# Accumulating DMAs in place of GpSimd additions in a channel attention with a rational feed-forward network

## The chip, the core and the metric

The kernel runs on one NeuronCore of one Trainium2 chip. The engines are named as the profile names them: PE is TensorE (matmuls), PEld its weight loads, DVE is VectorE, ACT is ScalarE, POOL is GpSimd, SP is SyncE, which here only issues DMAs. The metric is the time of one execution on the device, in microseconds (us).

## The reference

Two parts follow one another. For each of 4 batches with 6080 rows of 256 channels, a channel attention is computed, and its 24320 output rows then pass a feed-forward network whose activation is a quotient of two polynomials:

```python
qn = q / (norm(q, axis=1) + 1e-06);  kn = k / (norm(k, axis=1) + 1e-06)   # norms over the 6080 rows
s = kn.transpose(0, 2, 1) @ qn / tau                                       # 256 x 256 per batch
a = softmax(s);  x = (v @ a).reshape(24320, 256)
h = x @ w_in                                                               # 24320 x 2048
P = a0 + a1 * h + a2 * h**2 + a3 * h**3
Q = 1 + abs(b0) * abs(h) + abs(b1) * h**2
out = (P / (Q + 1e-06)) @ w_out                                            # 24320 x 256
```

## The kernel before

**Tiles.** The rows go in groups of 512 (the last of each batch has 448): 12 groups in each of 4 batches, 48 in all. The 2048 hidden channels go in 8 pairs of 128-channel blocks, pair 0 to pair 7, so there are 384 steps "group and pair" (function `pair`, line 620). The softmax matrix of a batch is multiplied into `w_in` first (`fuse`, line 560), so that h comes straight from v.

**One pair.** PE makes h of 256 channels by 512 rows into a PSUM tile `hx` (three such tiles, `hx0` to `hx2`) with 12 matmuls, called mm1 here. Then, with all tiles 128 x 1024:

- ACT "first": d = hx squared. POOL "line": d = d * |b1| + 1. ACT "second": uu = |b0 * hx|. POOL "sum": d = d + uu. That is the denominator Q. In pairs 1, 3 and 6 (`FACTORED`, line 252) it is made in another way, without a sum: ACT "first" uu = |b1 * hx|, DVE a product, ACT "abs", and later POOL "one", which adds the 1.
- ACT "slope": uu = a3 * hx + a2; DVE twice makes the numerator in hx ("num1", "num2").
- ACT "root" and "square": r = 1/d to the precision of the table. POOL "again": d = d * r. DVE "quot": hx = hx * r; DVE "last": g = (2 - d) * hx, a step of Newton's method. Only then is the hx tile free for the mm1 of another pair.
- PE multiplies g with `w_out` into `acc` (4 matmuls with two records each, in two halves), called the out product here; at the end of a group DVE turns acc and SP stores it.

**The attention of batch 0** stands at the start (24 halves of 256 rows of k and q: load, PE products, ACT square into one of two tiles `sq`, addition of the squares into one tile by POOL or DVE). The attention of batches 1 to 3 is spread over the pairs of the batch before (`Attn.half`, line 423); 12 halves of batch 1, called fronts, are pulled into the start. There POOL adds each square tile into `ssq` (line 464). The softmax of a batch (line 475) needs the finished ssq.

**What sets the order.** Every step is given to a planner (`Planner`, line 83) with an engine, a cost, what it reads and writes, and a due time: the step's row of `LAG` or `TIME` (lines 21 to 45) on top of 3.576 us per pair. The planner replays the engines and puts on each, whenever it is free, the ready step with the smallest due time. What comes out is a fixed order on each engine; on the chip each engine runs its rows in that order and waits for semaphores. So a new number in the table can reorder all five engines. There are also three hx, four d, four uu, three r, four g and two sq tiles; a step that needs a new tile waits until one is free.

Of the kernel before, what the change touches and what calls it, by code (L numbers as in the profile page):

```python
# [14 lines left out]
ALU = mybir.AluOpType  # L15
# [3 lines left out]


LAG = {
    "first": (0.84, 4.52, 2.78, 3.73, 4.53, 2.33, 3.41, 3.6),
    "prod": (-11.23, -0.03, -11.23, 6.14, -11.23, -11.23, 5.27, -11.23),
    "abs": (-35.28, -33.04, -35.28, -60.18, -35.28, -35.28, -12.39, -35.28),
    "line": (-60.83, 30.85, 1.23, -9.96, -64.93, -61.3, 25.68, -3.97),
    "second": (3.47, 5.1, 5.85, 6.25, 8.47, 6.18, 3.15, 4.97),
    "sum": (-75.1, -80.53, -59.16, -66.42, -83.56, -73.41, -47.34, -36.63),
    "slope": (6.9, 4.95, 7, 7.41, 9.07, 6.95, 6.12, 6.22),
    "num1": (80.21, 21.96, 120.89, 23.72, 98.59, 65.28, 53.4, 94.99),
    "num2": (91.21, 77.02, 48.39, 83.69, 132.26, 79.9, 92.26, 66.3),  # L30
    "root": (-17.03, -9.24, -6.87, -5.73, -6.19, -9.62, -12.27, -14.71),
    "one": (18.62, -22.45, 18.62, 2.61, 18.62, 18.62, 25.53, 18.62),
    "square": (-78.86, -34.07, -129.08, -42.44, -147.95, -117.98, -7.49, -107.82),
    "again": (-10.9, -52.88, -8.31, -23.6, -7.9, 6.38, -36.31, -6.49),
    "quot": (38.4, 26.11, 35.76, 10.27, 43.7, 29.95, 4.71, 41.91),
    "last": (-3.36, 0.17, -3.01, -4.4, 0.77, 1.56, -1.89, -4.37),
    "out": (24.58, 54.15, 41.53, 45.99, 18.94, 61.33, 13.35, 15.28),
    "in": (-5.72, -5.59, -3.14, -6.52, -2.09, -4.66, -7.12, -10.04), "in_n": 0,
}
TIME = {  # L40
    "pair": 3.576, "start": 61.026, "load": 1.674, "softmax": 52.628, "in": 4.243, "late_in": 1.499,
    "out0": 30.295, "out": 5.035, "attn0_0": -1.487, "attn_0": 1.155, "attn0": 4.026, "attn": 1.97,
    "attn1": 91.474, "value": 54.159, "fuse": 1.698, "finish": 21.052, "front": 41.363,
    "front_pace": 1.762, "ahead": 15.518, "vhi": 26.968, "vlo": 25.086,
}


# [29 lines left out]


class Step:
    __slots__ = ("eng", "cost", "fn", "key", "need", "after", "new", "bufs", "banks", "port", "n")  # L80


class Planner:
# [14 lines left out]
        self.slots, self.fifo, self.banks = slots, fifo, banks  # L98
        self.steps = []

    def add(self, eng, cost, key, fn, reads=(), writes=(), port=False):
        s = Step()
        s.eng, s.cost, s.fn, s.key = eng, cost, fn, key
# [24 lines left out]
        for w in before.values():  # L128
            w.after.append(s)
        self.steps.append(s)  # L130
        return s

    def order(self):
# [29 lines left out]
        while left:  # L163
            for e in ready:
                while busy[e] <= now and ready[e]:
                    skipped, pick = [], None
                    while ready[e]:
                        entry = heapq.heappop(ready[e])
                        if fits(entry[2]):
                            pick = entry[2]  # L170
                            break
                        skipped.append(entry)
                    for entry in skipped:
                        heapq.heappush(ready[e], entry)
                    if pick is None:
                        break
                    for b in pick.new:
                        b.slot = free[b.tag].pop(0)
                        if b.tag in queue:
                            queue[b.tag].pop()  # L180
                    out.append((now, pick))
                    left -= 1
                    busy[e] = now + pick.cost
                    if pick.port:
                        other = "POOL" if e == "DVE" else "DVE"
                        busy[e] = max(now, port[other]) + pick.cost
# [11 lines left out]
            while events and events[0][0] <= now:  # L198
                _, what, _, s = heapq.heappop(events)
# [17 lines left out]
def tile_channel_attention_rational_ffn(  # L217
# [43 lines left out]
    pool = InOrder(tc, nc.gpsimd)  # L261
# [139 lines left out]
    class Attn:  # L401
# [21 lines left out]
        def half(self, i, at, both, sps):  # L423
# [3 lines left out]
            base, pn = groups[g]  # L427
# [31 lines left out]
            else:  # L459
# [160 lines left out]
    def pair(m, at, vparts, w, acc):  # L620
# [9 lines left out]
        def c(b):  # L630
            return b[:, :, :n]
# [21 lines left out]
        else:  # L653
# [121 lines left out]
```

## Time and profile before

| | us |
|---|---|
| median of 2 runs | 2647.04 |
| the two runs | 2646.86 and 2647.22 |
| span of the profiled execution | 2645.5 |

| engine | busy us | share of the span |
|---|---|---|
| PE | 2595.5 | 98% |
| DVE | 2259.8 | 85% |
| POOL | 2216.3 | 84% |
| ACT | 2124.2 | 80% |

The profiled execution's span runs from its first to its last instruction; the runs' times hold about 1.5 us more. The busy time of PE is modelled for pipelined matmuls. Issuing a DMA is not counted as busy. The profile gives tile names without their numbers, and nearly every instruction stands on one helper's line (L58), so rows are told apart by tile names. The views read here are the page's parts, the table of busy times by stretch, the chain of work that ended last, the timeline of an engine, and the list of DMA issues with their time to landing.

### The profile page before, as it was taken

How to read it: one execution, taken by the hardware profiler on the slowest of the kernel's cores; microseconds unless marked ns; L12 is line 12 of the kernel's file. 1: busy time of each engine (PE TensorE's matmuls, PEld its weight loads, DVE VectorE, ACT ScalarE, POOL GpSimd, SP SyncE). 2: the span in 40 equal slices, each digit the busy share in tenths (PEclk: the TensorE clock that was granted, in tenths of full speed). 3: DMA queues.
4: the chain of work that ended last, by engine and by line, in shares of the span. 5: the costliest groups of instructions: out<-in, count | busy, mean ns of one | idle time of the engine just before them, and what ended most of it. 6: DMA issues, size and time to landing. Idle time of an engine off the chain costs nothing.

```text
span 2645.5 us, 26474 instructions
## 1 busy us (share of the span) xinstructions
PE 2595.5 (98%) x8744; PEld 1651.8 (62%) x8744; DVE 2259.8 (85%) x2035; ACT 2124.2 (80%) x2179; POOL 2216.3 (84%) x1152
## 2 busy tenths in 40 slices
PE   7899999999999999999999999999999999999998
PEld 6656666666666666666666666665666566666665
DVE  6898888988978787888888878888897889889887
ACT  5688888888878778788878778778887888888886
POOL 6889888888778999788878899878885888888886
PEclk9899999999999999999999999999999999999999
DMA  9512311111112222211121222211111111111101
GB/s 306 153 25 64 68 19 25 23 17 24 17 35 53 48 65 53 48 24 17 23 40 16 49 68 51 46 25 17 23 25 17 18 22 24 22 18 25 23 9 15
DMA packets 457017, 109.76 MB, mean 41 GB/s; under 512 B 405168, under 2 KB 453808, under 8 KB 456880
## 3 DMA queue, kind: packets, MB, share of 16 engines
q1 hardware_dynamic: 456880, 108.07, 19.4%
q8 instruction: 69, 1.13, 0.2%
q14 instruction: 68, 0.56, 0.1%
HBM read 83.10 MB, written 24.90 MB: 41 GB/s over the span
## 4 chain that ended last, share of the span: by engine, by line
PE 88%; ACT 4%; DVE 3%; DMA 2%; issue 1%; POOL 1%; SPq 0%; DVEq 0%; ACTq 0%; POOLq 0%
PE acc L58 45%; PE hx L58 43%; ACT uu L58 1%; DVE hx L58 1%; DMA r<-in_k_dram 1%; ACT r L58 1%; ACT d L58 1%; POOL d L58 0%; DVE uu L58 0%; DMA r<-in_q_dram 0%; DMA kq<-in_k_dram 0%; SPq L58 0%; ACT sq L58 0%; DVE g L58 0%; POOL ssq L58 0%
## 5 line engine op out<-in xcount | busy, mean ns | idle before, releaser
L58 PE MATMUL acc<-g,w_out_sb 128*128 128x512 f32 (+1 forms) x3072 | 1349.7, 588 | 4.5 <-DVE orow L58 4.4
L58 POOL TENSOR_TENSOR d<-d,r 128x1024 f32<-128x1024 f32 (+1 forms) x384 | 906.5, 2364 | 166.9 <-ACT r L58 155.0
L58 PE MATMUL hx<-vhi,w 128*128 128x512 f32 (+1 forms) x3072 | 961.4, 420 | 7.4 <-DVE g L58 5.3
L58 PEld LDWEIGHTS acc<-g,w_out_sb 128*128 128x128 f32 x3072 | 581.2, 189 | 618.6 <-issue 592.4
L58 PEld LDWEIGHTS hx<-vhi,w 128*128 128x128 f32 x3072 | 578.2, 189 | 229.4 <-issue 94.3
L58 POOL TENSOR_TENSOR d<-d,uu 128x1024 f32<-128x1024 f32 (+1 forms) x243 | 575.6, 2369 | 35.0 <-ACT uu L58 20.5
L58 DVE TENSOR_TENSOR uu<-uu,hx 128x1024 f32<-128x1024 f32 (+1 forms) x384 | 462.4, 1204 | 149.9 <-ACT uu L58 148.8
L58 DVE SCALAR_TENSOR_TENSOR hx<-hx,coef,r 128x1024 f32<-128x1024 f32 (+1 forms) x384 | 489.2, 1275 | 111.3 <-ACT r L58 106.9
L58 ACT ACTIVATE d<-hx 128x1024 f32<-128x1024 f32 (+1 forms) x243 | 247.1, 1017 | 345.7 <-PE hx L58 338.6
L58 DVE SCALAR_TENSOR_TENSOR hx<-uu,coef,hx 128x1024 f32<-128x1024 f32 (+1 forms) x384 | 487.7, 1273 | 4.2
L58 DVE SCALAR_TENSOR_TENSOR g<-d,hx 128x1024 f32<-128x1024 f32 (+1 forms) x384 | 461.0, 1201 | 21.6 <-POOL d L58 15.0
L58 PE MATMUL hx<-vlo,w 128*128 128x512 f32 (+1 forms) x1536 | 473.7, 390 | 0.0
L58 ACT ACTIVATE uu<-hx,babs 128x1024 f32<-128x1024 f32 (+1 forms) x384 | 425.9, 1109 | 50.7 <-PE hx L58 50.7
L58 ACT ACTIVATE uu<-hx,coef 128x1024 f32<-128x1024 f32 (+1 forms) x384 | 461.4, 1201 | 1.3 <-DVE d L58 1.3
L58 ACT ACTIVATE r<-d 128x1024 f32<-128x1024 f32 (+1 forms) x384 | 405.4, 1056 | 20.2 <-POOL d L58 17.8
L58 ACT ACTIVATE r<-r 128x1024 f32<-128x1024 f32 (+1 forms) x384 | 405.2, 1055 | 6.8
L58 POOL TENSOR_SCALAR d<-d,babs 128x1024 f32<-128x1024 f32 (+1 forms) x243 | 272.2, 1120 | 133.8 <-ACT d L58 130.7
L58 PEld LDWEIGHTS hx<-vlo,w 128*128 128x128 f32 x1536 | 288.9, 188 | 60.7
L58 DVE SCALAR_TENSOR_TENSOR d<-uu,babs,hx 128x1024 f32<-128x1024 f32 (+1 forms) x141 | 178.2, 1264 | 33.7 <-ACT uu L58 33.4
L58 POOL TENSOR_SCALAR d<-d,ones 128x1024 f32<-128x1024 f32 (+1 forms) x141 | 157.5, 1117 | 36.7 <-ACT r L58 36.6
L58 POOL TENSOR_TENSOR ssq<-sq,ssq 128x1024 f32<-128x1024 f32 (+1 forms) x69 | 166.0, 2406 | 24.0 <-ACT sq L58 19.5
L58 ACT ACTIVATE d<-d 128x1024 f32<-128x1024 f32 (+1 forms) x141 | 146.8, 1041 | 9.8 <-DVE d L58 9.8
(82 smaller groups left out, 1119.1 us busy)
## 6 DMA issues: line engine op xcount, KB each, us to landing
vst<-in_v_dram SPq DMA_DIRECT2D x352, 64.0 KB, 2.3
out_dram<-orow SPq DMA_DIRECT2D x352, 64.0 KB, 2.0
kq<-in_k_dram SPq DMA_DIRECT2D x78, 256.0 KB, 3.8
kq<-in_q_dram SPq DMA_DIRECT2D x78, 256.0 KB, 4.2
d<-in_moe_w_in_dram SPq DMA_DIRECT2D x8, 512.0 KB, 7.0
r<-in_k_dram SPq DMA_DIRECT2D x10, 256.0 KB, 6.5
r<-in_q_dram SPq DMA_DIRECT2D x10, 256.0 KB, 6.5
d<-in_moe_w_out_dram SPq DMA_DIRECT2D x4, 512.0 KB, 8.2
```

Of the source, the lines that this page charges most:

```text
L58: ins = op(*args, **kwargs)
```

## The change

Two kinds of POOL additions become DMAs that POOL issues and that add their source to what stands in the destination: the sum of pairs 0 and 4 in every group (96 additions) and the additions of square tiles into ssq in batches 1 to 3 (69 additions). Both are 128 x 1024 in 32-bit, 512 KB (a group of 448 rows and the last two halves of a batch are a little smaller). The planner counts each of them with 1.0 on POOL, and lets its result be used 5.0 later (`SUM_LANDS`, passed as `tail`). All due times in `LAG` and `TIME` are new, so the order changes on every engine.

```diff
+    CARRIED = (0, 4)
+
+    SUM_LANDS = 5.0
...
-    def add(self, eng, cost, key, fn, reads=(), writes=(), port=False):
+    def add(self, eng, cost, key, fn, reads=(), writes=(), port=False, tail=0.0):
...
-                    heapq.heappush(events, (busy[e] + self.HOP[e], 1, pick.n, pick))
+                    heapq.heappush(events, (busy[e] + self.HOP[e] + pick.tail, 1, pick.n, pick))
                     for c, lat in enumerate(self.LAT[e].values()):
-                        heapq.heappush(events, (busy[e] + lat, 10 + c, pick.n, pick))
+                        heapq.heappush(events, (busy[e] + lat + pick.tail, 10 + c, pick.n, pick))
...
-                fn = lambda: e.tensor_tensor(total[:pn], sq[:pn], total[:pn], op=ALU.add)
-                step(*(("DVE", 1.2) if own else ("POOL", 2.38)), at + 2, fn, [sq, total], [total], True)
+                if first:
+                    fn = lambda: e.tensor_tensor(total[:pn], sq[:pn], total[:pn], op=ALU.add)
+                    step(*(("DVE", 1.2) if own else ("POOL", 2.38)), at + 2, fn, [sq, total], [total], True)
+                else:
+                    fn = lambda: pool.dma_start(out=total[:pn], in_=sq[:pn], accum_op=ALU.add)
+                    step("POOL", 1.0, at + 2, fn, [sq, total], [total], tail=SUM_LANDS)
...
-            fn = lambda: pool.tensor_tensor(c(d), c(d), c(kk), op=ALU.add)
-            step("POOL", 2.36 * s, at + LAG["sum"][p], fn, [d, kk], [d])
+            if p in CARRIED:
+                fn = lambda: pool.dma_start(out=c(d), in_=c(kk), accum_op=ALU.add)
+                step("POOL", 1.0, at + LAG["sum"][p], fn, [d, kk], [d], tail=SUM_LANDS)
+            else:
+                fn = lambda: pool.tensor_tensor(c(d), c(d), c(kk), op=ALU.add)
+                step("POOL", 2.36 * s, at + LAG["sum"][p], fn, [d, kk], [d])
```

Of the tables, two rows show the manner of the change:

```diff
-    "sum": (-75.1, -80.53, -59.16, -66.42, -83.56, -73.41, -47.34, -36.63),
+    "sum": (-76.15, -179.7, -63.44, -133.87, -63.68, -59.31, -81.78, -42.08),
-    "pair": 3.576, "start": 61.026, "load": 1.674, "softmax": 52.628, "in": 4.243, "late_in": 1.499,
+    "pair": 3.576, "start": 69.136, "load": 1.731, "softmax": 58.346, "in": 3.756, "late_in": 1.499,
```

**Place 1, the middle of batch 0, where one group's pair 7 and the next group's pair 0 stand together.** On POOL before, with pair 7 in d3 and pair 0 in d0: line and sum of 7, line of 0, a split of the next group's values (vlo), sum of 0, again of 7, again of 0.

```order
L58 TENSOR_SCALAR d3_84<-d3_84,babs_77 128x1024
L58 TENSOR_TENSOR d3_84<-d3_84,uu0_85 128x1024
L58 TENSOR_SCALAR d0_81<-d0_81,babs_77 128x1024
L58 TENSOR_TENSOR vlo0_139<-cv0_97,vhi0_137 128x1024
L58 TENSOR_TENSOR d0_81<-d0_81,uu1_86 128x1024
L58 TENSOR_TENSOR d3_84<-d3_84,r1_108 128x1024
L58 TENSOR_TENSOR d0_81<-d0_81,r2_109 128x1024
```

On POOL now, with pair 0 in d3 and pair 7 in d0:

```order
L59 TENSOR_SCALAR d3_84<-d3_84,babs_77 128x1024
L59 TENSOR_SCALAR d0_81<-d0_81,babs_77 128x1024
L59 DMA d3_84<-uu0_85 128x1024
L59 TENSOR_TENSOR d0_81<-d0_81,uu3_88 128x1024
L59 TENSOR_TENSOR vlo0_139<-cv0_97,vhi0_137 128x1024
L59 TENSOR_TENSOR d0_81<-d0_81,r1_108 128x1024
L59 TENSOR_TENSOR d3_84<-d3_84,r2_109 128x1024
```

The sum of pair 0 has become a DMA and has moved ahead of the sum of pair 7; the landing has the sum of 7, vlo and the again of 7 beside it. On ACT before, the second of pair 0 (`uu1<-hx1,babs`) and its root (`r2<-d0`) have five rows between them:

```order
L58 ACTIVATE uu1_86<-hx1_91,babs_77 128x1024
L58 ACTIVATE r1_108<-d3_84 128x1024
L58 ACTIVATE uu3_88<-hx1_91,coef_71 128x1024
L58 ACTIVATE r1_108<-r1_108 128x1024
L58 ACTIVATE uu0_85<-hx2_92,babs_77 128x1024
L58 ACTIVATE uu2_87<-hx2_92,coef_71 128x1024
L58 ACTIVATE r2_109<-d0_81 128x1024
```

On ACT now, the second of pair 0 (`uu0<-hx2,babs`) and its root (`r2<-d3`):

```order
L59 ACTIVATE d3_84<-hx2_92 128x1024
L59 ACTIVATE uu3_88<-hx1_91,babs_77 128x1024
L59 ACTIVATE d0_81<-hx1_91 128x1024
L59 ACTIVATE uu0_85<-hx2_92,babs_77 128x1024
L59 ACTIVATE uu1_86<-hx2_92,coef_71 128x1024
L59 ACTIVATE uu2_87<-hx1_91,coef_71 128x1024
L59 ACTIVATE vhi0_137<-cv0_97 128x1024
L59 ACTIVATE r1_108<-d0_81 128x1024
L59 ACTIVATE uu3_88<-hx0_90,babs_77 128x1024
L59 ACTIVATE r1_108<-r1_108 128x1024
L59 ACTIVATE r2_109<-d3_84 128x1024
L59 ACTIVATE d1_82<-d1_82 128x1024
```

Now six rows stand between them, among them the root and square of pair 7, and the second of pair 0 comes only after the second and first of pair 7.

**Place 2, PE at the same joint.** Before, what follows the mm1 of pair 0 in a group of batch 0 (g and w_out_sb mark out products; x4 is a whole one, x2 a half): half an out product, the mm1 of pair 1, two and a half out products, and then the mm1 of pair 2 and of pair 3, which takes over the hx tile of pair 0.

```order
L58 MATMUL acc0_89<-g0_93,w_out_sb_80 128x512 x2
L58 MATMUL hx2_92<-vhi0_137,w1_117 128x512 x2
L58 MATMUL hx2_92<-vlo0_139,w1_117 128x512 x2
L58 MATMUL hx2_92<-vhi0_137,w21_127 128x512 x2
L58 MATMUL hx2_92<-vhi0_137,w1_117 128x512 x2
L58 MATMUL hx2_92<-vlo0_139,w1_117 128x512 x2
L58 MATMUL hx2_92<-vhi0_137,w21_127 128x512 x2
L58 MATMUL acc0_89<-g0_93,w_out_sb_80 128x512 x2
L58 MATMUL acc0_89<-g3_96,w_out_sb_80 128x512 x4
L58 MATMUL acc0_89<-g1_94,w_out_sb_80 128x512 x4
```

Now the mm1 of pair 0 of the next group is followed by the mm1 of pair 7 of this one (not shown), then by these rows, then by the mm1 of pair 2 and of pair 3, which again takes over the hx tile of pair 0:

```order
L59 MATMUL acc0_89<-g2_95,w_out_sb_80 128x512 x2
L59 MATMUL acc0_89<-g3_96,w_out_sb_80 128x512 x2
L59 MATMUL hx0_90<-vhi1_138,w1_117 128x512 x2
L59 MATMUL hx0_90<-vlo1_140,w1_117 128x512 x2
L59 MATMUL hx0_90<-vhi1_138,w21_127 128x512 x2
L59 MATMUL hx0_90<-vhi1_138,w1_117 128x512 x2
L59 MATMUL hx0_90<-vlo1_140,w1_117 128x512 x2
L59 MATMUL hx0_90<-vhi1_138,w21_127 128x512 x2
L59 MATMUL acc0_89<-g3_96,w_out_sb_80 128x512 x2
L59 MATMUL acc0_89<-g0_93,w_out_sb_80 128x512 x4
L59 MATMUL acc0_89<-g1_94,w_out_sb_80 128x512 x4
```

One mm1 and half an out product have come between pair 0's mm1 and pair 3's: before three mm1 and three out products, now four mm1 and three and a half.

**Place 3, POOL at the start.** Now the additions of the fronts (ssq) and the first pairs stand like this; each ssq row reads and writes the same tile as the one before it:

```order
L59 DMA ssq0_142<-sq1_106 128x1024
L59 TENSOR_TENSOR vlo0_139<-cv0_97,vhi0_137 128x1024
L59 DMA ssq0_142<-sq0_105 128x1024
L59 DMA ssq0_142<-sq1_106 128x1024
L59 TENSOR_SCALAR d0_81<-d0_81,babs_77 128x1024
L59 DMA d0_81<-uu0_85 128x1024
L59 DMA ssq0_142<-sq0_105 128x1024
L59 TENSOR_SCALAR d1_82<-d1_82,babs_77 128x1024
L59 DMA ssq0_142<-sq1_106 128x1024
L59 TENSOR_TENSOR d0_81<-d0_81,r0_107 128x1024
```

Before, the eleven additions of the fronts were POOL work of the same kind as its other additions; now each row is a DMA, and a row that adds into ssq waits on POOL for the landing of the one before it.

## Rows read from the trace of the kernel before

**Rows 1.** The page, part 1: span, and busy time of PE.

```profile
span 2645.5 us, 26474 instructions
PE 2595.5 (98%) x8744; PEld 1651.8 (62%) x8744; DVE 2259.8 (85%) x2035; ACT 2124.2 (80%) x2179; POOL 2216.3 (84%) x1152
```

**Rows 2.** Busy time by stretch: stretch, length, each engine's, PE clock, DMA share, GB/s.

```profile
0.00:57.20 57.20, 43.88 (x184) 35.80 (x184) 40.18 (x57) 31.12 (x34) 39.47 (x24) 1.00 0.97 305
57.20:114.40 57.20, 46.24 (x186) 37.57 (x186) 50.88 (x69) 37.83 (x50) 41.16 (x18) 0.91 0.74 226
114.40:171.60 57.20, 50.43 (x159) 32.01 (x159) 49.69 (x46) 42.19 (x46) 53.00 (x27) 0.91 0.12 19
...
sum 2637.20, PE 2594.85 PEld 1651.75 DVE 2258.68 ACT 2124.22 POOL 2216.33; mean PE 185.35 PEld 117.98 DVE 161.33 ACT 151.73 POOL 158.31
```

**Rows 3.** The chain that ended last, one group: start, length, engine, tile, count.

```profile
2182.53 5.49 PE hx L58 x24
2188.03 3.43 PE acc L58 x8
...
2231.94 5.49 PE hx L58 x24
```

**Rows 4.** The page, part 5: costliest groups, busy, mean ns, idle before, its releaser.

```profile
L58 POOL TENSOR_TENSOR d<-d,r 128x1024 f32<-128x1024 f32 (+1 forms) x384 | 906.5, 2364 | 166.9 <-ACT r L58 155.0
L58 POOL TENSOR_TENSOR d<-d,uu 128x1024 f32<-128x1024 f32 (+1 forms) x243 | 575.6, 2369 | 35.0 <-ACT uu L58 20.5
...
L58 DVE SCALAR_TENSOR_TENSOR g<-d,hx 128x1024 f32<-128x1024 f32 (+1 forms) x384 | 461.0, 1201 | 21.6 <-POOL d L58 15.0
...
L58 POOL TENSOR_TENSOR ssq<-sq,ssq 128x1024 f32<-128x1024 f32 (+1 forms) x69 | 166.0, 2406 | 24.0 <-ACT sq L58 19.5
```

**Rows 5.** Timeline of ACT at the joint of pairs 7 and 0: start, length.

```profile
2189.25 1.13 ACT L58 ACTIVATE uu<-hx,babs 128x1024 f32<-128x1024 f32 x1
2190.24 1.23 ACT L58 ACTIVATE uu<-hx,coef 128x1024 f32<-128x1024 f32 x1
2191.33 1.09 ACT L58 ACTIVATE r<-d 128x1024 f32<-128x1024 f32 x1
2192.28 1.09 ACT L58 ACTIVATE vhi<-cv 128x1024 fp32r<-128x1024 f32 x1
2193.23 1.09 ACT L58 ACTIVATE r<-r 128x1024 f32<-128x1024 f32 x1
2194.24 1.11 ACT L58 ACTIVATE uu<-hx,babs 128x1024 f32<-128x1024 f32 x1
2195.25 1.05 ACT L58 ACTIVATE r<-d 128x1024 f32<-128x1024 f32 x1
```

**Rows 6.** DMA issues, 800 to 1750 us: count, KB each, median us to landing.

```profile
kq<-in_k_dram SPq DMA_DIRECT2D x38, 256.0 KB, 3.5
kq<-in_q_dram SPq DMA_DIRECT2D x38, 256.0 KB, 3.9
...
vst<-in_v_dram SPq DMA_DIRECT2D x128, 64.0 KB, 2.3
```

**Rows 7.** Timeline of SP's queue: start and length of two issues.

```profile
870.45 0.37 SPq L58 DMA_DIRECT2D kq<-in_k_dram  x1
870.87 0.46 SPq L58 DMA_DIRECT2D kq<-in_q_dram  x1
```

**Rows 8.** The page, part 6: DMA issues of 512 KB at the start.

```profile
d<-in_moe_w_in_dram SPq DMA_DIRECT2D x8, 512.0 KB, 7.0
...
d<-in_moe_w_out_dram SPq DMA_DIRECT2D x4, 512.0 KB, 8.2
```

**Rows 9.** The chain at the start: additions of two fronts on it.

```profile
90.54 2.45 POOL ssq L58
...
93.06 2.70 POOL ssq L58
```

**Rows 10.** Timeline of POOL at the start: front additions ahead of sums.

```profile
105.83 2.36 POOL L58 TENSOR_TENSOR ssq<-sq,ssq 128x1024 f32<-128x1024 f32 x1 [0.82 <-ACT sq L58]
108.14 2.81 POOL L58 TENSOR_TENSOR d<-d,uu 128x1024 f32<-128x1024 f32 x1
...
112.20 2.34 POOL L58 TENSOR_TENSOR ssq<-sq,ssq 128x1024 f32<-128x1024 f32 x1
```

More of the change, by code (lines that the diff above doesn't have):

```diff
@@ L21 @@
 LAG = {
[L22 to L26, printed above, removed]
-    "sum": (-75.1, -80.53, -59.16, -66.42, -83.56, -73.41, -47.34, -36.63),
-    "slope": (6.9, 4.95, 7, 7.41, 9.07, 6.95, 6.12, 6.22),
-    "num1": (80.21, 21.96, 120.89, 23.72, 98.59, 65.28, 53.4, 94.99),
@@ L30 @@
[L30 to L36, printed above, removed]
@@ L37 @@
-    "out": (24.58, 54.15, 41.53, 45.99, 18.94, 61.33, 13.35, 15.28),
-    "in": (-5.72, -5.59, -3.14, -6.52, -2.09, -4.66, -7.12, -10.04), "in_n": 0,
+    "first": (-1.99, 4.49, 3.1, 3.03, 1.87, -0.28, 3.36, 6.44),
+    "prod": (-11.23, -0.46, -11.23, -0.12, -11.23, -11.23, 3.8, -11.23),
+    "abs": (-35.28, -29.57, -35.28, -8.58, -35.28, -35.28, -17.35, -35.28),
+    "line": (-122.86, 33.27, 8.62, 16.73, -76.41, -61.41, 66.33, -3.06),
+    "second": (3.74, 8.46, 5.21, 2.29, 3.83, 1.92, 2.25, 3.66),
@@ new lines @@
+    "sum": (-76.15, -179.7, -63.44, -133.87, -63.68, -59.31, -81.78, -42.08),
+    "slope": (5.31, 7.08, 5.75, 6.91, 4.8, 5.34, 5.4, 10.51),
+    "num1": (66.19, 42.24, 127.36, 40.45, 114.89, 112.9, 108.9, 121.16),
+    "num2": (64.16, 106.31, 36.31, 113.96, 151.19, 73.39, 60.59, 112.92),
+    "root": (-5.53, -6.36, -6.67, -4.44, -5.9, -3.77, -5.84, -3.96),
+    "one": (18.62, -13.08, 18.62, 46.24, 18.62, 18.62, 50.45, 18.62),
+    "square": (-78.24, -15.43, -115.55, -80.53, -183.43, -168.21, 8.84, -69.8),
@@ L39 @@
+    "again": (26.08, -26.07, -56.72, -85.22, 42.66, 72.65, 12.44, 42.65),
+    "quot": (-16.24, 29.72, 73.49, 15.23, 90.25, 57.13, 41.36, 1.68),
+    "last": (-3.16, -5.28, -5.96, -8.65, -11.31, -12.32, -9.08, -1.92),
+    "out": (-7.39, 43.1, 31.6, 151.13, 23.05, 33.84, 45.58, 72.14),
+    "in": (-12.17, -4.89, -0.56, -3.35, -0.62, -3.21, -5.76, -8.02),
+    "in_n": 0,
 }
 TIME = {
-    "pair": 3.576, "start": 61.026, "load": 1.674, "softmax": 52.628, "in": 4.243, "late_in": 1.499,
-    "out0": 30.295, "out": 5.035, "attn0_0": -1.487, "attn_0": 1.155, "attn0": 4.026, "attn": 1.97,
@@ L43 @@
-    "attn1": 91.474, "value": 54.159, "fuse": 1.698, "finish": 21.052, "front": 41.363,
-    "front_pace": 1.762, "ahead": 15.518, "vhi": 26.968, "vlo": 25.086,
+    "pair": 3.576, "start": 69.136, "load": 1.731, "softmax": 58.346, "in": 3.756, "late_in": 1.499,
+    "out0": -35.671, "out": 8.872, "attn0_0": -1.138, "attn_0": 1.117, "attn0": 4.621,
+    "attn": 1.914, "attn1": 91.638, "value": 56.407, "fuse": 2.088, "finish": 22.037,
+    "front": 55.516, "front_pace": 2.35, "ahead": -13.72, "vhi": 33.796, "vlo": 0.862,
@@ L79 @@
 class Step:
-    __slots__ = ("eng", "cost", "fn", "key", "need", "after", "new", "bufs", "banks", "port", "n")
+    __slots__ = ("eng", "cost", "tail", "fn", "key", "need", "after", "new", "bufs", "banks", "port", "n")
 class Planner:
@@ L99, in __init__ @@
         self.steps = []
-    def add(self, eng, cost, key, fn, reads=(), writes=(), port=False):
+    def add(self, eng, cost, key, fn, reads=(), writes=(), port=False, tail=0.0):
         s = Step()
-        s.eng, s.cost, s.fn, s.key = eng, cost, fn, key
+        s.eng, s.cost, s.fn, s.key, s.tail = eng, cost, fn, key, tail
         s.n = len(self.steps)
@@ L289, in buf, with step @@
         return Buf(tag, view)
-    def step(eng, cost, key, fn, reads=(), writes=(), port=False):
+    def step(eng, cost, key, fn, reads=(), writes=(), port=False, tail=0.0):
         new = [b for b in writes if b.tag is not None and not b.writers]
@@ L297, in run @@
             fn()
-        plan.add(eng, cost, key, run, reads, writes, port)
+        plan.add(eng, cost, key, run, reads, writes, port, tail)
     ident = const.tile([P, P], F32, name="ident")
```

## The prediction

> **What bounds the kernel now.** I read the page's busy times first: PE has work for 2595.5 of 2645.5 us, 98% [rows 1]. Then the busy times by stretch, to see where the rest lies: up to 2637.2 us PE is busy for 2594.85, so 42.4 us are idle, and 31.1 of these fall in the first 171.6 us (13.3, 11.0 and 6.8) [rows 2]. There the clock counts too: in the second and third stretch the granted clock was 0.91 of 2.4 GHz, that is, some of the time at 1.2 GHz; 0.09 of 114.4 us is 10.3 us [rows 2]. Behind the start, 11.3 us are left for 2465 us. Then the chain that ended last, for what a group costs when PE never waits: 12 matmuls of mm1 take 5.49 / 2 = 2.75 us, an out product 3.43, and from one "hx x24" to the same place a group later it is 2231.94 - 2182.53 = 49.41 us [rows 3]; 8 x (2.75 + 3.43) = 49.4. The steady groups are pure PE work. So POOL is not the bound; taking work off it brings nothing there, and the change can gain only at the start and lose anywhere.
>
> **What it removes.** 96 sums at 2.369 us are 227 us, the 69 additions into ssq are 166 us [rows 4]: 393 of POOL's 2216 us [rows 1]. In the steady groups this goes at no gain, since PE covers it. At the start it counts: two front additions stand on the chain itself, 2.45 + 2.70 us [rows 9], and two more stand ahead of the sums of the first pairs, 2.36 + 2.34 us [rows 10], whose end the first out products wait for. If each of these four becomes an issue of 1 us, 9.9 - 4 = 6 us come off the start. I add 3 us for first pairs that begin earlier because POOL reaches them earlier, a choice; the bound above is 41 us, idle and clock together. Gain at the start: 9 us.
>
> **What it adds: issues.** The trace has no DMA issued by POOL. The nearest rows are SP's issues, 0.37 and 0.46 us [rows 7]; the other end is the addition that the issue replaces, 2.37 us [rows 4]. I take 1.0, nearer to SP's: 165 us in all, beside PE.
>
> **What it adds: the landing.** L is the time from the start of an issue to the landing. No row shows an adding DMA. From below: two transfers of 256 KB, issued 870.87 - 870.45 = 0.42 us apart [rows 7], land 3.5 and 3.9 us after their issues [rows 6], so 512 KB are there after 4.3 us. From above: 512 KB took 7.0 and 8.2 us at the start, where the DMA engines are 97% busy [rows 2, 8]. An adding DMA also has to fetch what it adds to. From 64 KB in 2.3 us to 256 KB in 3.5 us [rows 6] is 1.2 us per 192 KB, or 3.2 us per 512 KB; with all of it on top L is 7.5, with half of it 5.9. I take 5.9 plus 0.6 for POOL's slower issue: 6.5 us. The ends are 4.3 and 8.2.
>
> **How much landing pair 0 can hide.** At the joint of the groups (place 1) I set t = 0 at the start of pair 0's mm1. Its mm1 and that of pair 7 end at 5.5 [rows 3]. ACT then has three rows, second 7, first 7, second 0, at about 1.0 each (2190.24 - 2189.25 is 0.99) [rows 5], plus the overlap of the last: 8.5. POOL issues at 8.6. Six ACT rows stand before the root of pair 0: two slopes (1.09 from start to start), vhi, root 7 (0.95 each), first 1 and square 7 (1.01 each): 6.1 us [rows 5]. Root 7 needs the sum of 7, which POOL ends at 8.6 + 1.0 + 2.37 = 12.0, while ACT reaches root 7 at 11.6; so the root of pair 0 could start at 8.5 + 6.1 + 0.4 = 15.0. A landing up to L = 15.0 - 8.6 = 6.4 holds nothing up. Behind it stand root, abs and square (0.95 + 1.0 + 1.06), again 2.36 and last 1.20 [rows 4, 5] and 0.3 of hand-overs: hx is free at 21.9. Pair 3 needs it after four mm1 and three and a half out products (place 2): 4 x 2.75 + 3.5 x 3.43 = 23.0. So 1.1 us are spare, and **PE begins to wait at L = 7.5**. Before, the same joint gave 3 x (2.75 + 3.43) = 18.5 us, with a sum of 2.4 us in it: the new order has bought 4.5 us for a landing that is 4 us longer. Pair 4 I take as no tighter.
>
> A sentence of the Trainium skill speaks against this: "Collectives: The Full Stack", section "The bandwidth ceiling", says that a reduction in the DMA path is slower than a copy because it reads two sources through one ring, which halves its rate. As an estimate by that page, the data part would double, L would be 7.5 + 0.6 = 8.1 instead of 6.5, and the sum would be about 2690 (48 x 0.6 + 11 x 1.6 more); no trace shown here has such a DMA, so this stays open and belongs to the first rival below.
>
> **The sum.** With L = 6.5 the steady groups cost nothing. At the start, the fronts' additions hang on one another (place 3): each waits on POOL for the landing before it, with a loaded DMA queue around it [rows 2], and both sq tiles are held as long. I charge 4 us for this, four landings late by 1 us. 2645.5 - 9 + 4 = 2640.5 in the span, and with the 1.5 us that the runs hold beyond it **2642 us** (the median before is 2647.04).
>
> **Rivals.**
>
> 1. *The landing is late at pair 0 (slower).* PE is the bound, so each us of L over 7.5 is lost once per group: 48 x (L - 7.5). ACT, which runs in order, stands at the root of pair 0, and behind it stand the abs of pair 1 and the first of pair 2; DVE and then PE wait for those. The eleven additions of the fronts add up to 11 x (L - 6.5). At 8.2, the upper end: 34 + 19 = 53, so 2695. 2% is passed at about L = 8.3. For it: the 7.0 and 8.2 us of the loaded queue [rows 8]. Against: behind 171.6 us the queue is nearly empty, and 512 KB took 4.3 us there. Chance 0.22, of which 0.05 between 7.5 and 8.3 us.
> 2. *The start gives back what it gains.* All eleven landings at the start late by 1 us, or ACT held at a full sq tile as before: 2642 + 9, 2651. For it: the DMA share of 0.97 and 0.74 [rows 2]. Against: the fronts now stand further apart. Chance 0.20.
> 3. *POOL is not relieved.* An issue costs as much as the addition, 2.4 us. Then the sum of 7, its root and with them the root of pair 0 come 1.4 us later, hx is free at 23.3 against 23.0, 0.3 x 48 = 14 us, and the 6 us of the start are gone too: 2662. Chance 0.05.
>
> **How the numbers follow.** The forecast has 0.53. About 2% (53 us) is what a measurement of this kernel can tell from no change. Faster by that would need all 42.4 us of idle time and the 10.3 us of the clock, 0.01. Slower takes the part of rival 1 beyond L = 8.3, 0.17. Same is the rest, 0.82. The range goes from 2618 (a start better by three times the 9 us, without the 4) to 2700, just past rival 1 at the upper end of L; beyond 2700 lie about 0.17. The forecast's own range is 2630 to 2652.
>
> **What would show it right or wrong.** POOL's busy time should fall to about 1820 us. The list of DMA issues should show the DMAs of POOL landing in a median of 5.5 to 7.5 us; this is the step on which all rests. PE busy by stretch should stay without idle time behind 172 us, and a group should take 49.4 us in the chain. If rival 1 holds, PE waits for DVE's last in every group, ACT's root waits for a DMA, and the group takes 49.4 + (L - 7.5). If rival 3 holds, the sum of 7 begins over 2 us after the issue ahead of it. The forecast is wrong at the start if the steady part begins later than 172 us, or if POOL stands at ssq rows there for longer than the 5 us that it stood on the chain.

## The result, and the profile after

The changed kernel takes 2684.84 us (median of 2 runs, 2684.07 and 2685.61) against 2647.04: a ratio of 1.0144, with a 95% interval of 1.0114 to 1.0173. It is 37.8 us slower, where 5 us less were forecast. The profiled execution has a span of 2682.3 us; its granted clock is 0.995, as in the one before, so the clock has no part in the difference. The page after, part 1, the groups of part 5 that answer to [rows 4], and the DMA issues of POOL in part 6:

```profile
span 2682.3 us, 26401 instructions
PE 2607.8 (97%) x8744; PEld 1648.3 (61%) x8744; DVE 2253.9 (84%) x2035; ACT 2134.4 (80%) x2179; POOL 1976.6 (74%) x1152
...
L59 PE MATMUL hx<-vhi,w 128*128 128x512 f32 (+1 forms) x3072 | 975.3, 423 | 23.6 <-DVE g L59 22.6
...
L59 DVE SCALAR_TENSOR_TENSOR g<-d,hx 128x1024 f32<-128x1024 f32 (+1 forms) x384 | 462.2, 1205 | 104.0 <-POOL d L59 64.7
...
L59 POOL TENSOR_TENSOR d<-d,uu 128x1024 f32<-128x1024 f32 (+1 forms) x147 | 363.2, 2471 | 7.3
...
d<-uu POOLq DMA_DIRECT2D x88, 512.0 KB, 5.1
ssq<-sq POOLq DMA_DIRECT2D x63, 512.0 KB, 5.0
```

The table of groups by line gives the two kinds of DMAs on POOL (busy, mean ns, idle before and its releasers):

```profile
L59 POOL DMA_DIRECT2D d<-uu x96 | 87.3, 909 | 25.5 <-POOL d L59 18.8 <-ACT uu L59 3.1 <-ACT r L59 2.7
L59 POOL DMA_DIRECT2D ssq<-sq x69 | 63.4, 919 | 56.4 <-DMA ssq<-sq 26.4 <-ACT sq L59 24.3 <-ACT r L59 5.6
```

The prices came out well: an issue costs POOL 0.91 us, the adding DMA lands a median of 5.0 to 5.1 us after its issue. This page counts the issues of POOL as busy, other than was said of DMA issues ahead of the prediction; without them, POOL has 1976.6 - 87.3 - 63.4 = 1825.9 us of work. And yet DVE's last waits 104.0 us where it waited 21.6 [rows 4], and PE's mm1 waits 22.6 us for DVE's last (5.3 on the page before).

Where the time went is seen by stretches. The end of a stretch is the moment at which DVE starts to turn acc (orow<-acc) of its last group; lengths in us, from the traces of the two kernels and of three runs described below:

| groups | what they hold | before | after | e10 | e2 | e12 |
|---|---|---|---|---|---|---|
| 0 to 9 | start, steady part of batch 0 | 654.2 | 654.7 | 652.9 | 676.2 | 671.4 |
| 10 to 18 | attention of batch 2, batch 0 to 1 | 500.8 | 504.0 | 502.5 | 524.8 | 506.9 |
| 19 to 21 | steady, batch 1 | 148.3 | 148.6 | 148.5 | 151.8 | 148.6 |
| 22 to 30 | attention of batch 3, batch 1 to 2 | 501.4 | 504.8 | 503.1 | 524.4 | 506.0 |
| 31 to 33 | steady, batch 2 | 148.3 | 148.5 | 148.6 | 152.0 | 148.8 |
| 34 to 36 | batch 2 to 3 | 158.8 | 170.3 | 168.2 | 174.7 | 170.2 |
| 37 to 45 | steady, batch 3 | 444.7 | 459.5 | 446.7 | 469.0 | 459.5 |
| 46, 47 | end | 81.4 | 84.1 | 83.5 | 84.6 | 84.2 |

After against before: 14.8 us in the steady groups of batch 3, 11.5 at the change from batch 2 to 3, 3.2 + 3.4 in the two stretches with attention, 2.7 at the end, 0.5 at the start. Stretches with the same rows differ between executions: e10 has the rows of the changed kernel up to group 35, and its start is 1.8 us shorter, its two stretches with attention 1.5 and 1.7. So only part of the 3.2 and the 3.4 is clear of that. The steady groups of batches 0 to 2 have kept their time (49.5 us), those of batch 3 have gone from 49.41 [rows 3] to 51.05.

So batch 3 was read first. One joint of pairs 7 and 0 there, POOL's timeline (start, length; idle before and its releaser in brackets): line 7, the DMA of pair 0, sum 7, vlo, again 7, again 0.

```profile
2210.45 1.12 POOL L59 TENSOR_SCALAR d<-d,babs 128x1024 f32<-128x1024 f32 x1 [2.25 <-ACT d L59]
2211.91 0.88 POOL L59 DMA_DIRECT2D d<-uu  x1 [0.34 <-POOL d L59]
2212.55 2.65 POOL L59 TENSOR_TENSOR d<-d,uu 128x1024 f32<-128x1024 f32 x1
2214.88 2.62 POOL L59 TENSOR_TENSOR vlo<-cv,vhi 128x1024 fp32r<-128x1024 f32 x1
2218.37 2.38 POOL L59 TENSOR_TENSOR d<-d,r 128x1024 f32<-128x1024 f32 x1 [0.87 <-ACT r L59]
2221.15 2.39 POOL L59 TENSOR_TENSOR d<-d,r 128x1024 f32<-128x1024 f32 x1 [0.40 <-ACT r L59]
```

ACT's timeline at the same joint, second 7, root 7 and the root of pair 0:

```profile
2208.33 1.11 ACT L59 ACTIVATE uu<-hx,babs 128x1024 f32<-128x1024 f32 x1 [1.70 <-PE hx L59]
...
2215.23 1.06 ACT L59 ACTIVATE r<-d 128x1024 f32<-128x1024 f32 x1 [0.73 <-POOL d L59]
...
2218.13 1.04 ACT L59 ACTIVATE r<-d 128x1024 f32<-128x1024 f32 x1
```

DVE's timeline, the last of pair 7 and the turn of acc:

```profile
2220.78 1.22 DVE L59 SCALAR_TENSOR_TENSOR g<-d,hx 128x1024 f32<-128x1024 f32 x1 [0.98 <-POOL d L59]
...
2231.84 1.28 DVE L59 SCALAR_TENSOR_TENSOR d<-uu,babs,hx 128x1024 f32<-128x1024 f32 x1
2233.04 1.24 DVE L59 STREAM_TRANSPOSE orow<-acc 128x1024 f32<-128x1024 f32 x1
```

And PE's timeline: the end of pair 7's mm1, half an out product, (the mm1 of pair 1,) two and a half out products, and the mm1 of pair 2, which takes over the hx tile of pair 7; then the out product of the next group's pair 0:

```profile
2207.67 0.62 PE L59 MATMUL hx<-vhi,w 128*128 128x512 f32 x2
2208.13 1.88 PE L59 MATMUL acc<-g,w_out_sb 128*128 128x512 f32 x4
...
2212.61 8.74 PE L59 MATMUL acc<-g,w_out_sb 128*128 128x512 f32 x20
2222.06 0.73 PE L59 MATMUL hx<-vhi,w 128*128 128x512 f32 x2 [0.70 <-DVE g L59]
...
2234.34 5.42 PE L59 MATMUL acc<-g,w_out_sb 128*128 128x512 f32 x12 [0.29 <-DVE orow L59]
```

Line 7 ends at 2211.57, but sum 7 starts only at 2212.55, 0.98 us later: the issue of pair 0's DMA stands in between. Root 7 waits 0.73 us for sum 7; again 7, last 7 and the mm1 of pair 2 are late in turn, and PE waits 0.70 us. DVE is then busy, but for 0.2 us, up to the turn of acc, which ends late too, and PE waits 0.29 us more. In the chain that ended last, the mm1 right behind the first wait takes 3.03 instead of 2.77 us and the out products right behind the second 5.42 instead of 5.15. Together that is 0.70 + 0.26 + 0.29 + 0.27 = 1.52 of the 1.64 us that the group has grown.

### The profile page after: what moved, and what is told of

Its sections match the earlier page's. It is cut to its first block, busy times and chain, and to the rows that moved or that the text cites. A ratio compares the mean times of both kernels' runs of the same rounds, so it can differ in the third digit from the quotient of the medians.

```text
span 2682.3 us, 26401 instructions
## 1 busy us (share of the span) xinstructions
PE 2607.8 (97%) x8744; PEld 1648.3 (61%) x8744; DVE 2253.9 (84%) x2035; ACT 2134.4 (80%) x2179; POOL 1976.6 (74%) x1152
## 4 chain that ended last, share of the span: by engine, by line
PE 75%; ACT 7%; POOL 5%; DVE 4%; issue 4%; DMA 4%; SPq 1%; POOLq 0%; DVEq 0%; ACTq 0%
PE hx L59 38%; PE acc L59 37%; POOL d L59 4%; ACT uu L59 3%; ACT r L59 2%; DVE g L59 1%; ACT d L59 1%; DMA kq<-in_q_dram 1%; DVE hx L59 1%; DMA ssq<-sq 1%; DVE orow L59 1%; DMA r<-in_q_dram 1%; POOL orow L59 1%; SPq L59 1%; DVE d L59 0%
## 5 line engine op out<-in xcount | busy, mean ns | idle before, releaser
L59 PE MATMUL hx<-vhi,w 128*128 128x512 f32 (+1 forms) x3072 | 975.3, 423 | 23.6 <-DVE g L59 22.6
L59 DVE SCALAR_TENSOR_TENSOR g<-d,hx 128x1024 f32<-128x1024 f32 (+1 forms) x384 | 462.2, 1205 | 104.0 <-POOL d L59 64.7
L59 ACT ACTIVATE uu<-hx,coef 128x1024 f32<-128x1024 f32 (+1 forms) x384 | 455.0, 1201 | 15.4 <-DVE d L59 13.0
L59 ACT ACTIVATE r<-d 128x1024 f32<-128x1024 f32 (+1 forms) x384 | 400.8, 1046 | 60.5 <-POOL d L59 50.0
L59 POOL TENSOR_TENSOR d<-d,uu 128x1024 f32<-128x1024 f32 (+1 forms) x147 | 363.2, 2471 | 7.3
L59 POOL TENSOR_SCALAR d<-d,ones 128x1024 f32<-128x1024 f32 (+1 forms) x141 | 165.3, 1172 | 123.8 <-ACT r L59 123.8
L59 PE MATMUL hx<-kq 128*128 128x256 f32 (+1 forms) x576 | 133.5, 385 | 10.5 <-DMA kq<-in_q_dram 9.1
```

What stands on the lines that cost most here:

```text
L59: ins = op(*args, **kwargs)
```

## The experiments

Three theories stood at the start. **A:** the issue ahead of the sum of 7 delays pair 7, whose hx tile PE needs first. **B:** the landing, 5.1 us where the addition took 2.4, holds the hx tiles of pairs 0 and 4 too long. **C:** the new order is slower by itself, with or without DMAs. All kernels below compute the whole reference.

**e1: the DMA behind the sum of 7** (`sums[m]` is the step that makes the sum of pair m):

```diff
     steps = plan.order()
+    for G in range(37, TG):
+        dma, add = sums[G * NFP], sums[G * NFP - 1]
+        i, j = steps.index(dma), steps.index(add)
...
+        steps.insert(j, steps.pop(i))
```

> The changed kernel, with one move: in the joints of batch 3 (11 of them) the DMA of pair 0 stands behind the sum of pair 7 on POOL instead of ahead of it. Theory A (the issue ahead of the sum of 7 is what costs: it starts 0.98 us late and takes 2.65 instead of 2.37, so pair 7 holds its hx tile 16.6 us where PE has only 15.8 us of other work): the hold of pair 7 falls to about 15.4, the group of batch 3 from 51.05 to 49.5 us, the total by 11 x 1.5 to about 2668. Theory B (the longer landing fills the three hx tiles): the landing of pair 0 comes 2.1 us later, about 1 us behind the place where ACT now starts its root; the group stays at 51 or grows, 2685 to 2695. Theory C (the new order itself is slow, with or without DMAs): 2685, no change.

Measured: 2682.53 us, ratio 1.0133 (1.0118 to 1.0149); the group of batch 3 stays at 51.1. POOL's timeline of e1 at the joint shows sum 7, the issue and vlo:

```profile
2212.14 2.40 POOL L59 TENSOR_TENSOR d<-d,uu 128x1024 f32<-128x1024 f32 x1
2214.47 0.87 POOL L59 DMA_DIRECT2D d<-uu  x1
2215.11 2.64 POOL L59 TENSOR_TENSOR vlo<-cv,vhi 128x1024 fp32r<-128x1024 f32 x1
```

ACT's timeline of e1 shows second 7 and the root of pair 0:

```profile
2208.81 1.11 ACT L59 ACTIVATE uu<-hx,babs 128x1024 f32<-128x1024 f32 x1 [1.70 <-PE hx L59]
...
2219.33 1.06 ACT L59 ACTIVATE r<-d 128x1024 f32<-128x1024 f32 x1 [1.46 <-DMA d<-uu]
```

PE's waits of e1 in four groups of batch 3 (total us, times, longest):

```profile
PE acc L59 <- DVE orow L59: 2.1, 4, 0.5
PE hx L59 <- DVE g L59: 0.3, 1, 0.3
```

Theory A had the first half right: sum 7 starts at once, and PE's wait for its hx tile has gone (2.8 us in four groups of the changed kernel; the 0.3 that are left in e1 are at the mm1 of pair 3, which takes over the tile of pair 0). But the issue now comes 2.1 us later behind second 7 (2214.47 - 2208.81 against 2211.91 - 2208.33), ACT stands at the root of pair 0 for 1.46 us until the landing, everything behind it is late, and the turn of acc holds PE instead. A alone is refuted: in this order of the other rows there is room at the joint for the issue or for the landing, not for both.

**e2: the same order, with additions.**

```diff
-                fn = lambda: pool.dma_start(out=c(d), in_=c(kk), accum_op=ALU.add)
+                fn = lambda: pool.tensor_tensor(c(d), c(d), c(kk), op=ALU.add)
...
-                    fn = lambda: pool.dma_start(out=total[:pn], in_=sq[:pn], accum_op=ALU.add)
+                    fn = lambda: pool.tensor_tensor(total[:pn], sq[:pn], total[:pn], op=ALU.add)
```

> The changed kernel's order on every engine, but each of the 165 DMAs is a POOL addition again. Theory A: the row ahead of the sum of 7 now takes 2.37 instead of 0.98 us, pair 7 holds its tile 1.1 us longer (without the slowing of 0.28), the group of batch 3 goes to 52.2 and batches 0 to 2 begin to wait too: about 2700 to 2730. Theory B (landing): without the landing the time falls back to about 2647 to 2655. Theory C (order): about 2685, as changed.

Measured: 2767.53 us, ratio 1.0455 (1.0437 to 1.0472); the group of batch 3 takes 52.1 us, that of batch 0 50.6. The group of batch 3 is what A said (52.2), as sum 7 now has 2.37 us ahead of it; the whole is 37 us above its range. B, which saw the time fall back without the landing, is refuted as the only cause. The new order with additions is 120 us slower than before, and the DMAs win 83 of these back: it was planned with 1.0 us on POOL for each of the moved rows. PE's waits in four groups of batch 3 of e2:

```profile
PE hx L59 <- DVE g L59: 7.0, 4, 1.7
PE acc L59 <- DVE orow L59: 1.2, 4, 0.3
```

**e3 and e4: the tables and the DMAs apart, each planned anew.** e3 has the new tables with additions in code and planner (`CARRIED = ()`, and the branch of `first` for every batch). e4 has the tables of before with the DMAs in code and planner.

> The new due times alone: no DMA in the code or in the planner, which plans anew with the new tables and additions of 2.36 and 2.38 us on POOL. Theory C (the new tables are worse by themselves): 2670 or more. Theories A and B (the DMAs cost): about 2647, with a group of batch 3 at 49.4 to 49.6 us.

> The DMAs alone: the due times of the kernel before, with both kinds of DMAs in the code and in the planner (1.0 on POOL, 5.0 to the use). With these tables the sum of 7 stands ahead of the DMA of pair 0 in the middle of a batch. Theory A: no issue stands ahead of the sum of 7, so no loss there: 2645 to 2655. Theory B: the landing is 2.7 us longer than the addition in pairs 0 and 4 of every group, and the places where hx is taken over had 0.05 to 3.3 us to spare in batch 3; about 2 us a group are lost, 2700 or more. Theory C: 2647, as before.

Measured: e3 2896.35 us, ratio 1.0939 (1.0922 to 1.0955); e4 2826.69, ratio 1.0676 (1.0660 to 1.0692). No theory had said this of both. Planned anew, neither table suits the other kernel's costs: in e3 the steady group of batch 3 takes 54.6 us, in e4 about 53.5. These two do not tell DMAs from order, since the order differs from both kernels; the next ones keep the order of before.

**e5, e6, e7: the order of before, with both kinds of DMAs, with ssq's alone, and with those of the pairs alone.** The planner counts as before, so every engine runs the rows of before; only what POOL executes differs:

```diff
                 fn = lambda: e.tensor_tensor(total[:pn], sq[:pn], total[:pn], op=ALU.add)
+                if not first:
+                    fn = lambda: pool.dma_start(out=total[:pn], in_=sq[:pn], accum_op=ALU.add)
...
             fn = lambda: pool.tensor_tensor(c(d), c(d), c(kk), op=ALU.add)
+            if p in (0, 4):
+                fn = lambda: pool.dma_start(out=c(d), in_=c(kk), accum_op=ALU.add)
```

> The kernel before with its order on every engine kept; only the 165 additions run as DMAs in their places. Theory B (the landing of 5.1 us where an addition took 2.4 keeps hx of pairs 0 and 4 about 2.7 us longer): in batch 3 the tiles of pairs 0 and 4 stood free for 1.56 and 0.83 us before their next mm1, so 1.1 + 1.9 = 3 us a group, about 2647 + 45 x 3 = 2780. Theory C (the new order, not the DMAs, is what costs): 2640 to 2655.

> The kernel before in its own order, with only the 69 additions into ssq as DMAs. If the landings of these are hidden, as the prediction took them: the start gains up to 6 us and nothing else moves, 2641 to 2647. If they are not: a row that adds into ssq waits on POOL for the landing of the one ahead of it, up to 4 us, and the sums of pairs behind it are late: 2650 to 2700.

> The kernel before in its own order, with only the 96 sums of pairs 0 and 4 as DMAs. Theory B: the steady group of batch 3 grows from 49.41 by about 3 us to 52.4, and the whole is near 2780, no less than with both kinds of DMAs by more than 30 us. Theory C: 2647.

Measured: e5 2870.34 us, ratio 1.0853 (1.0833 to 1.0874); e6 2690.25, ratio 1.0165 (1.0150 to 1.0180); e7 2800.43, ratio 1.0577 (1.0561 to 1.0592). C is refuted as the only cause: in the old order the DMAs cost 223 us. That is 90 us more than B worked out for e5. Part of it may be the clock: the runs of e5 were granted 0.973 to 0.980 and those of e3 0.969 to 0.971, those of before 0.993 to 0.996; the share of the loss that this makes was not separated. The page of e5 shows how, ACT's root at the landing and PE behind DVE's last (idle before, and what ended it):

```profile
L58 PE MATMUL hx<-vhi,w 128*128 128x512 f32 (+1 forms) x3072 | 958.2, 419 | 121.3 <-DVE g L58 112.9
...
L58 ACT ACTIVATE r<-d 128x1024 f32<-128x1024 f32 (+1 forms) x384 | 401.6, 1047 | 226.3 <-DMA d<-uu 202.3
```

The total of e7 is within 20 us of what B worked out, but it lies 70 us below e5, where B allowed 30, and the places are not B's: the steady groups of batch 3 take 50.2 to 50.9 us, not 52.4, and those of batch 0 51.9 to 56.5. e6 shows a cost of its own. Of its 43 us, 37 are there by the end of group 0 (its turn of acc is at 219.8, before 182.6). POOL's timeline of e6 at the start, the fronts' additions one behind the other:

```profile
86.35 0.86 POOL L58 DMA_DIRECT2D ssq<-sq  x1 [6.16 <-DMA ssq<-sq]
92.50 0.86 POOL L58 DMA_DIRECT2D ssq<-sq  x1 [5.29 <-DMA ssq<-sq]
98.66 0.86 POOL L58 DMA_DIRECT2D ssq<-sq  x1 [5.30 <-DMA ssq<-sq]
104.79 0.86 POOL L58 DMA_DIRECT2D ssq<-sq  x1 [5.27 <-DMA ssq<-sq]
```

Each waits on POOL until the one before it has landed, so they follow at 6.15 us where additions follow at 2.4, and POOL does nothing else in between.

The four combinations of order and operation, in us:

| | additions | DMAs |
|---|---|---|
| order of before | 2647.04 | 2870.34 (e5) |
| new order | 2767.53 (e2) | 2684.84 (after) |

The new order hides 185 of the 223 us that the DMAs cost in the old one. The 38 that are left are the result.

**e8: the joint without issue and without landing.** In batch 3 alone, the sum of pair 0 is an addition behind the sum of 7, and vlo is moved out of the way behind the again of pair 0:

```diff
+                if p == 0 and m // NFP in JOINTS:
+                    fn = lambda: pool.tensor_tensor(c(d), c(d), c(kk), op=ALU.add)
...
+    for G in JOINTS:
+        behind(sums[G * NFP], sums[G * NFP - 1])
+        i, j = steps.index(sums[G * NFP - 1]), steps.index(again[G * NFP])
+        for x in [x for x in steps[i:j] if x in low]:
+            behind(x, again[G * NFP])
```

(`JOINTS` is `range(37, TG)`, `low` holds the steps of vlo, and `behind(x, y)` puts step x right behind y.)

> The changed kernel; in the 11 joints of batch 3 alone the sum of pair 0 is a POOL addition again, behind the sum of pair 7, and the split of the next values (vlo) stands behind the again of pair 0. So neither does an issue stand ahead of the sum of 7, nor has the root of pair 0 a landing to wait for. If the joint of pairs 7 and 0 is what lengthens the groups of batch 3: a group of 49.4 to 49.6 us instead of 51.05, 11 x 1.5 = 17 us off, about 2668. If the order of the other rows does (DVE, pair 4): 50.5 or more, 2680 to 2685.

Measured: 2673.47 us, ratio 1.0100 (1.0085 to 1.0115), a group of 50.5 us: between the two expectations. In PE's waits of e8 only the turn of acc is left, in each of four groups:

```profile
PE acc L59 <- DVE orow L59: 2.1, 4, 0.5
```

In its chain the turn stands behind the last of pair 1, whose again comes late; on POOL vlo now stands ahead of it. So the experiment itself probably put part of this wait there. The next two runs separate this.

**e9: the turn of acc first, and e10: joint and turn together.** e9 changes one row per group on DVE in batch 3. e10 has this, the sum of pair 0 as in e8, and vlo behind the sum of pair 2, where POOL stood idle for 2.3 us:

```diff
+    for G in JOINTS:
+        if G < TG - 1:
+            behind(prods[G * NFP + 3], turns[G - 1])
```

> The changed kernel with one move on DVE in batch 3: the turn of acc (orow) stands ahead of the product of pair 3 instead of behind it, 1.2 us earlier. If the joint and the turn each add their own wait of PE (0.70 and 0.29 us in the trace of the changed kernel): PE no longer waits for orow, the group goes from 51.05 to about 50.5, 11 x 0.5 = 6 us off, about 2679. If the joint alone sets the length of the group: no change, 51.0 and 2685.

> The changed kernel with three edits in batch 3: the sum of pair 0 an addition behind the sum of pair 7 (as in the run of the joint), the split vlo moved on behind the sum of pair 2, where POOL stands idle, and orow ahead of the product of pair 3. If the joint and what is queued behind it on DVE are all that lengthens batch 3: a group of 49.4 to 49.6 us, 11 x 1.55 = 17 us off, 2662 to 2668. If something else in the new order (the landing of pair 4) still holds PE: 50 or more, 2670 and up.

Measured: e9 2679.09 us, ratio 1.0119 (1.0105 to 1.0133), a group of 50.5; e10 2666.65, ratio 1.0076 (1.0061 to 1.0092), a group of 49.63. Both are as expected, e10 at the upper end. In e9 PE's wait for the turn is gone and that for pair 7's tile has stayed:

```profile
PE hx L59 <- DVE g L59: 2.8, 4, 0.7
```

In e10 the list of PE's waits over four groups of batch 3 is empty. So the steady groups of batch 3 are explained but for 0.2 us a group: the joint of pairs 7 and 0, and the turn of acc queued behind it. (e10 takes away issue and landing together; e1 has shown that each of them can hold PE there.) Of 14.8 us, 12.8 are back in groups 37 to 45, and 2 more in group 36. That is what the experiments explain of the 37.8 us; the rest was not tried. The DMA of pair 4 is still in e10, so it costs next to nothing there.

**e11: DMAs only where they were seen to help.** In e6 two groups (17 and 29) were faster than before, 52.4 against 54.3 us.

```diff
+                if self.b >= 2 and i >= 8:
+                    fn = lambda: pool.dma_start(out=total[:pn], in_=sq[:pn], accum_op=ALU.add)
```

> The kernel before in its own order, with the additions into ssq as DMAs only in batches 2 and 3 and only from their ninth half on (32 of 69). With all 69 as DMAs the last groups of attention took 52.4 instead of 54.3 us in two batches, and the losses lay at the start and where several landings followed one another at a batch's beginning. If both hold here: 2 x 1.9 = 3.8 us off, 2643, and nothing lost elsewhere. If the landings ahead of the softmax cost: 2647 to 2652.

Measured: 2643.29 us (median of 11 runs), ratio 0.9984 (0.9976 to 0.9993). It is the fastest of all, by 4 us. Groups 17 and 29 take 52.38 and 52.34 us, where before took 54.27 and 54.25, and the other stretches are as before but for the start, which is 1.4 us shorter in this trace although its rows are the same. Before, the chain went through ACT's square, POOL's addition into ssq and the fold on DVE to DVE's last at this place, and in the 70 us around it PE waited 2.0 us for DVE's last; in e11 it waits

```profile
PE hx L58 <- DVE g L58: 0.3, 1, 0.3
```

**e12: the new order with only the DMAs of the pairs.** The edit is the ssq half of that of e2.

> The changed kernel's order on every engine, with the sums of pairs 0 and 4 as DMAs and the 69 additions into ssq as POOL additions again. All additions in this order took 2767.5, all DMAs 2684.8. If the DMAs of the pairs are what this order was made for: about 2690 to 2700, the ssq rows only adding up to 1.5 us each beside PE. If the ssq rows need to be short in it: 2720 or more.

Measured: 2705.65 us, ratio 1.0221 (1.0207 to 1.0234), between the two expectations. Additions into ssq cost 20.8 us in the new order, 16 of them by the end of group 2. The DMAs of the pairs carry most of the gain over e2 (62 of 83 us), those of ssq the rest, most of it at the start.

## Why the prediction was wrong, step by step

**What bounds the kernel, and what is removed: right.** PE is still the bound, POOL lost 390 us of work (forecast 393), and nothing in the steady part became faster for it.

**The issue: right.** 1.0 us was taken, 0.91 is the mean after.

**The landing: too long, on the safe side.** 6.5 us was taken from the range 4.3 to 8.2; it is 5.0 to 5.1, and 4.7 to 5.3 in e5 to e7. Most of what I put on top for the fetching of the destination was not there, if the other two terms hold. So the landing, "the step on which all rests", came out below the 5.5 to 7.5 us that were expected of it, and the time was missed all the same. From the rule of the Trainium skill in "Collectives: The Full Stack", section "The bandwidth ceiling", I had estimated 8.1; that estimate did not come true, but no run here has a plain copy of this size from SBUF to SBUF, so whether an adding DMA runs at half its rate stays open. The Trainium skill's page "DMA: Bandwidth & Descriptors", section "Anatomy of one DMA — SWDGE (gpsimd) path", gives a fit of 2.0 us plus the bytes by 436 GB/s, which as an estimate is 3.2 us for 512 KB; the median landing after the change, 5.1 us, is 1.9 us above that.

**Pair 0: right where I looked.** A landing of 5.1 lies below the 7.5 from which PE should wait at pair 0, and in the middle of batch 0 the group grew by only 0.1 us. The spare time in front of ACT's root of pair 0 was put at 6.4 - 6.5, that is none at all for the forecast L, and 1.3 us for the L measured; at the joint of batch 3 shown above it is 0.9, since the DMA issued at 2211.91 lands 5.3 us later and the root starts at 2218.13. In e1, with an issue 2.1 us later behind second 7, the root waits 1.46.

**"With L = 6.5 the steady groups cost nothing": the step that failed.** The steady groups of batch 3 cost 14.8 us. The sentence rested on one hx tile at one joint of one batch. Two things were left out.

- *Pair 7.* The working had its times: sum 7 ends at 12.0, delayed by the issue. From there root, first 1 and square (3.0 us), again (2.36), last (1.20) and hand-overs (0.3) free its tile at 18.9, or 16.1 after the start of its mm1 at 2.75. I did not ask when PE wants that tile.
- *Batch 3.* Its order is another. It is the one batch with no attention of a next batch in it; that is not a difference of the groups compared here, since the steady groups of batches 0 to 2 hold no attention rows either. In the middle of batch 0 there are two mm1, its own and that of pair 1, and three and a half out products from the start of pair 7's mm1 to that of pair 2: 2 x 2.75 + 3.5 x 3.43 = 17.5 us, and 16.1 fit. In batch 3 there are three out products: 15.8, and 16.1 do not fit. In the trace the hold is 16.6 us (as worked out ahead of e1), and the 0.70 us of PE are this. The turn of acc behind it, at the end of DVE's run, adds its own wait. e10 takes both away and has a group of 49.63.

**"Pair 4 I take as no tighter": right by luck,** as e10 shows with it in place.

**The changes of batch: never looked at.** They cost 11.5 us from batch 2 to 3, and 3.2 + 3.4 in the two stretches with attention. Of the 11.5 us, 2 belong to the joint, as e10 shows in group 36. The change from 2 to 3 takes 170.2 us in e12, so the landings into ssq are not what costs there, and 174.7 in e2, where nothing lands but POOL's rows are longer. In the old order the DMAs of the pairs alone lengthen it too, from 158.8 to 174.1 us (e7). So the cause stays open between the order and the DMAs of the pairs; what follows is argued from the trace and was not tried. The chain after, at the point where PE waits longest for an hx tile, goes through the softmax's rows on DVE (e), with the last of a pair behind them:

```profile
2006.40 1.05 DVE e L59
...
2007.47 2.20 DVE e L59
...
2009.70 1.12 DVE e L59
...
2011.19 1.09 DVE g L59
...
2012.33 2.72 PE hx L59 x12
```

Behind it, the products with `w_in` for batch 3, each of which needs an hx tile of its own, are spread from 2028 to 2067 us; before, they stood close together, from 2027 to 2045.

**The start: no gain where 5 us were forecast.** Group 2's turn of acc comes at 308.5 us (308.0 before); in e1, e8, e9 and e10, whose rows are the same up to there, at 306.5, 304.4, 308.2 and 306.2, and in e11, with the rows of before up to there, at 306.6. So no gain is clear of the differences between executions. Of the 9 us of relief 3 were a choice. The 4 us charged for landings that wait on one another look too small: up to 184 us POOL waits 11.0 us for landings ahead of ssq rows, more than the 5 us that the prediction named as its sign of being wrong, and e6 shows the same rows at a price of 37 us where the order does not spread them. This is what rival 2 says of the start, but the start holds only 0.5 of the 37.8 us.

**The rivals.** Rival 1 named a late landing at pair 0: not by its own condition (L stayed far below 7.5), though e1 shows that 2 us more at this place would have been enough to make ACT wait. Rival 3 had the mechanism, "the sum of 7, its root" later, but only for an issue of 2.4 us and only as far as it reached pair 0; e2 comes nearest to that case, at 1.05 us a group more than after the change in batch 3. What happened is a fourth case between them: the cheap issue, at the pair that was not priced.

**The range** of 2618 to 2700 held the time, on the strength of a rival that did not come about: that is luck. It is luck too that the change stays under 2%, to which 0.82 was given: its interval lies wholly on the side that was not forecast. (The lower end, 2618, is a span; as a time of a run it would be 2620.) Of the signs, PE's waits for DVE's last came, but not in every group; ACT's root waits, but mostly for POOL (50.0 of its 60.5 us on the page after) and not for a DMA.

## What to carry to other kernels

An operation that is moved off a busy engine and takes longer from start to end has to be checked at every place where a scarce buffer is taken over, in each stretch that has an order of its own: for each pair that stands beside the moved row, when its tile is free against when it is wanted. A shorter row can still be dear if it stands ahead of a row that another chain waits for. An order, or a table of due times, made for one set of costs does not carry to another: e2 to e5, which mix them, are 5 to 9% slower than before. So the DMAs and the order can be tried apart only with the order kept fixed.

## What the runs showed of the hardware

- An adding DMA of 512 KB from SBUF to SBUF takes POOL 0.87 to 0.92 us to issue (means of after, e5 and e6) and lands 4.5 to 5.3 us from the issue (medians for 512 KB in all kernels that have them); the longest after the change took 9.2 us, into ssq.
- Such DMAs into one tile follow one another at 6.15 us (e6), two and a half times the addition that they replace.
- The issue and the next instruction of POOL overlap in the records: sum 7 starts 0.64 us after the issue of 0.88 and is shown with 2.65. From the issue's start to the end of vlo it is 5.59 us, which is 0.88 plus the 4.71 that two such additions took in a row without an issue ahead (e8). So at this place the traffic of the DMA did not slow POOL's own work next to it.
- The loads of k and q land later in the kernel with both kinds of DMAs, in medians of 4.5 and 5.0 us against 3.8 and 4.2; with one kind alone (e6, e7, e12) they take 3.9 to 4.0 and 4.1 to 4.3.
